# Two preparation steps of the weights, issued on GpSimd or on ScalarE

## The chip, the cores and the metric

One core of a Trainium2 chip runs the whole kernel. Its engines work side by side, each in the order of its own queue: TensorE (PE in the profile, with its weight loads as PEld), VectorE (DVE), ScalarE (ACT), GpSimd (POOL) and SyncE (SP), which issues the DMAs. They wait for each other by semaphores. The metric is the device time of one execution in microseconds (us): the median of the runs shown.

## The reference

Two stages follow each other on `x`, four batches of 12416 rows of 128. The first is attention through 32 inducing points, the second a gated feed-forward layer with 1536 inner columns:

```python
def mab(q, kv):
    s = scale * (q @ kv.transpose(0, 2, 1))
    s = s - s.max(-1, keepdims=True)
    a = np.exp(s)
    a /= a.sum(-1, keepdims=True) + 1e-09
    return a @ kv
h = mab(I, x)                 # the inducing rows look at x
y = mab(x, h)                 # x looks at them
g, val = y @ w_gate, y @ w_val
out = (g * (1.0 / (1.0 + np.exp(-g))) * val) @ w_out
```

All inputs and outputs are float32. Inside the kernel the three weights arrive as pairs of 32-bit words and are made into float32 on the chip.

## The kernel before

Since `y = a @ h`, the kernel multiplies the weights of gate and value by `h` first (32 rows a batch) and then runs them on the attention weights `a`. The output side is a product of a high and a low part, each of the type fp32r: three matmuls in L735 to L737 (`h_hi` with `wo_lo`, `h_hi` with `wo_hi`, `h_lo` with `wo_hi`).

The work after the first 66 us is a loop over slots (25 column groups of 12 tiles for each of the four batches). A slot has two matmuls into `gv` (L696, L697), the silu on ScalarE (L702), the product on VectorE (L710), the cast to `h_hi` (L718), the subtraction for `h_lo` (L720, mostly on GpSimd) and the three output matmuls of an earlier tile. The first column group of batch 0 (`whole`) is done differently: its output matmul is a single one in float32 (L732).

The change lies in what comes before that loop, from about 28 to 66 us, where the weights are made ready. They come in nine pieces of 512 columns: J0 to J5 for gate and value, o0 to o2 for the output. The class `Piece` (from L170) has one method for each step:

- `X` (L186, ScalarE) scales the high words into a work buffer `t`; `sh` (L189, VectorE) shifts and masks `t`; `jn` (L192, VectorE) joins in the sign bit and reads two operands from SBUF.
- `low` (L183) scales the low words by 2^-29, from uint32 to int32, in place with a step of two words.
- `add` (L195, GpSimd) adds `t` and the scaled low words as integers. The result is a piece of `wgv_sb`, or for o0 to o2 the float32 weight that L732 uses.
- For o0 to o2 only, `hi` (L198) casts that weight to `wo_hi` (fp32r), and `lo` (L201, GpSimd) subtracts it to give `wo_lo`.

The order of all this is written out by hand, in the string `SECOND` and the table `FIRST`. Each token is a call, and each engine runs its own instructions in the order of the tokens. The part that the prediction speaks of most:

```python
jn:J3 pa:2 f:2 g:1 add:o0 m:0 pk:2 X:J4 sum:1 f:3 pm:2 add:J3 rec:1 m:1 g:2 X:o1 k:0 pa:3 pc:2 g:3 low:J4 sh:J4 m:2 f:4 f:5 jn:J4 k:1 pk:3 sh:o1 g:4
m:3 no:1:1 pm:3 k:2 at:1 X:J5 sh:J5 pc:3 g:5 low:J5 jn:J5 low:o1 jn:o1 add:J4 pa:4 add:J5 f:6 m:4 pk:4 m:5 g:6 pb:4 k:3 f:7 pa:5 m:6 add:o1 ah:1:1 f:8
al:1:0 g:7 X:o2 pk:5 sh:o2 g:8 low:o2 k:4 pm:5 f:9 jn:o2 pc:5 k:5 f:10 sp:1 m:7 k:6 m:8 f:11 g:9 add:o2 k:7 m:9 g:10 g:11 m:10 m:11 hi:o0 lo:o0 hi:o1
```

The other tokens: `pa:i` is the matmul that projects piece Ji (L403, TensorE), with `pk`, `pb`, `pm` and `pc` (L406 to L417) to split the result; `f`, `g`, `m`, `k` are the matmuls, silu, product and output matmul (L732) of a tile of the first column group; `sum`, `rec`, `no` (L472, on GpSimd), `at`, `ah`, `al`, `sp` normalise the attention weights of the next group, transpose, split and spread them; `z0` to `z8` make the attention weights of the first group (L531 is `z5`, L541 is `z6`). `ld:o1` and `ld:o2` reload buffers that `add:J0` and `add:J1` have read.

Of the kernel before, what the change touches and what calls it, by code (L numbers as in the profile page):

```python
# [11 lines left out]
AF = mybir.ActivationFunctionType  # L12
ALU = mybir.AluOpType
AX = mybir.AxisListType
U32 = mybir.dt.uint32
I32 = mybir.dt.int32
# [94 lines left out]
def induced_set_attention_then_swiglu(ctx: ExitStack, tc: tile.TileContext, xt, xn, ind, wgv, wo, out):  # L111
    nc = tc.nc
# [49 lines left out]
    wo_hi = const.tile([P, DFF], F32R, name="wo_hi")  # L162
# [7 lines left out]
    class Piece:  # L170
# [9 lines left out]
            nc.sync.dma_start(out=raw, in_=(wo if k == "o" else wgv)[:, 2 * WP * i:2 * WP * i + 2 * WP].rearrange("p (n w) -> p n w", w=2))  # L180

        def low(self):
            nc.scalar.activation(out=self.lw.bitcast(I32), in_=self.lw, func=AF.Copy, scale=2.0 ** -29)  # L183

        def X(self):
            nc.scalar.activation(out=self.t.bitcast(F32), in_=self.hw.bitcast(F32), func=AF.Copy, scale=2.0 ** -112)  # L186
# [8 lines left out]
            nc.gpsimd.tensor_add(out=self.w.bitcast(I32), in0=self.t.bitcast(I32), in1=self.lw.bitcast(I32))  # L195

        def hi(self):
            nc.scalar.copy(out=wo_hi[:, self.cs], in_=self.w)  # L198

        def lo(self):  # L200
            nc.gpsimd.tensor_sub(out=wo_lo[:, self.cs], in0=self.w, in1=wo_hi[:, self.cs].bitcast(F32))  # L201
# [14 lines left out]
    def attention(b, one, xn0=None, xt0=None):  # L216
# [19 lines left out]
        def load_xt(q, lo=0, hi=None):  # L236
            if lo == 0:
                if xn0 is not None and q >= NXT and q not in st.xt:
                    st.xt[q] = xt0.tile([P, max(CH), NG, 32], F32, name="xt0")
                else:  # L240
                    st.xt[q] = xtp.tile([P, max(CH), NG, 32], F32, name="xt_sb")
            hi = CH[q] if hi is None else hi
            nc.sync.dma_start(
                out=st.xt[q][:, lo:hi],
                in_=xt[b, :, P * (CH0[q] + lo):P * (CH0[q] + hi)].rearrange("c (i j r) -> c i j r", j=NG, r=32))
# [10 lines left out]
        def load_xn(q, lo=0, hi=None):  # L256
            hi = CH[q] if hi is None else hi
            nc.sync.dma_start(out=rows(q)[:, lo:hi], in_=xn[b, :, CH0[q] + lo:CH0[q] + hi, :])
# [160 lines left out]
        def proj_round(i, ev=nc.vector.tensor_copy):  # L419

            weights()
            ps = ps_gv.tile([P, 512], F32, name="gv")
            for j in range(NG):
                at = PC * (NG * i + j)
                nc.tensor.matmul(out=ps[32 * j:32 * j + 32, :PC], lhsT=st.hT[:, 0:M], rhs=wgv_sb[:, at:at + PC], start=True, stop=True)  # L425
            hi, lo = [eTp.tile([P, W], F32R, name="eT")[:, :PC] for _ in range(2)]
            ev(out=hi, in_=ps[:, :PC])
            nc.vector.tensor_sub(out=lo, in0=ps[:, :PC], in1=hi.bitcast(F32))
            st.pw[i] = hi, lo
# [418 lines left out]
```

## Time and profile before

| what | us |
|---|---|
| median of 3 runs | 1397.06 (1396.88 to 1397.12) |
| the profiled execution | 1398.15 |
| its span in the trace | 1396.4 |
| PE busy | 1381.0 |
| ACT busy | 1254.6 |
| POOL busy | 1193.8 |
| DVE busy | 1184.5 |

The trace holds every instruction of one execution, with start and duration. The span runs from its first to its last instruction; the execution's own time is 1.75 us longer. Rows of groups give the line, engine, operation, output and inputs, shape, count, then the busy time in us and the mean in ns, then the idle time of the engine just before. Rows in order of time give the start and the duration in us. Rows of one line give the duration in ns as minimum, median and maximum. An instruction's start can lie a little before the end of the one before it on its engine, since they overlap.

### The profile page before, as it was taken

What the parts mean: (1) busy time and instruction counts of PE and PEld (TensorE: products, weight loads), DVE (VectorE), ACT (ScalarE), POOL (GpSimd) and SP (SyncE); (2) the same over time, 40 slices, a digit from 0 to 9 for tenths busy, and PEclk for the clock granted to TensorE, in tenths of its full rate; (3) what the DMA queues carried; (4) which work ended last, traced back from release to release, by engine and by line L of the source; (5) the groups of instructions that cost most, each with busy time, mean ns of one, the idle gap of its engine ahead of it and who ended that gap; (6) DMA issues with size and microseconds to landing.
All of it is one profiled execution on the core that took longest, in us unless ns stands there. A gap on an engine that the chain in (4) does not pass through costs nothing.

```text
span 1396.4 us, 24926 instructions
## 1 busy us (share of the span) xinstructions
PE 1381.0 (99%) x7452; PEld 1177.1 (84%) x7452; DVE 1184.5 (85%) x2080; ACT 1254.6 (90%) x2388; POOL 1193.8 (85%) x995
## 2 busy tenths in 40 slices
PE   8999999999999999999999999999999999999998
PEld 6577788889987887799998788789999888889998
DVE  5788878988888888988888878988888888888887
ACT  4888898889998898999999888799999999999997
POOL 1589868989998878899999878889989999999997
PEclk9999999999999999999999999999999999999999
DMA  9224432312133443121124424321111111111110
GB/s 368 86 75 151 161 111 95 112 55 72 39 119 114 143 137 117 51 74 38 41 60 128 145 85 139 110 73 56 41 43 45 33 44 46 34 45 40 43 43 22
DMA packets 50822, 119.80 MB, mean 86 GB/s; under 512 B 11392, under 2 KB 28288, under 8 KB 50688
## 3 DMA queue, kind: packets, MB, share of 16 engines
q1 hardware_dynamic: 50688, 118.22, 25.9%
q8 instruction: 59, 0.97, 0.3%
q14 instruction: 75, 0.61, 0.1%
HBM read 62.87 MB, written 25.43 MB: 63 GB/s over the span
## 4 chain that ended last, share of the span: by engine, by line
PE 92%; ACT 3%; DVE 2%; DMA 1%; issue 1%; POOL 0%; SPq 0%; DVEq 0%; ACTq 0%
PE gv L697 17%; PE o L737 17%; PE o L735 17%; PE gv L696 17%; PE o L736 17%; PE gv L275 2%; ACT h_hi L718 1%; ACT silu L702 1%; DMA xt<-xt 1%; PE o L323 1%; PE o L732 1%; DVE h L710 1%; PE o L275 1%; POOL h_lo L720 0%; PE gv L425 0%
## 5 line engine op out<-in xcount | busy, mean ns | idle before, releaser
L720 POOL TENSOR_TENSOR h_lo<-h,h_hi 128x512 fp32r<-128x512 f32 (+1 forms) x890 | 1098.1, 1258 | 153.8 <-ACT h_hi L718 100.1
L702 ACT ACTIVATE silu<-gv 128x512 f32<-128x512 f32 (+1 forms) x1200 | 705.2, 588 | 63.1 <-PE gv L696 54.5
L710 DVE TENSOR_TENSOR h<-gv,silu 128x512 f32<-128x512 f32 (+1 forms) x891 | 593.9, 668 | 149.6 <-ACT silu L702 86.1
L718 ACT CAST h_hi<-h 128x512 fp32r<-128x512 f32 (+1 forms) x788 | 476.8, 605 | 44.1 <-DVE h L710 34.5
L696 PE MATMUL gv<-stack,tw 128*128 128x512 f32 (+1 forms) x1200 | 453.8, 378 | 2.4 <-DVE stack L548 0.8
L697 PE MATMUL gv<-stack,tw 128*128 128x512 f32 (+1 forms) x1200 | 450.7, 376 | 3.6 <-ACT silu L702 1.8
L737 PE MATMUL o<-h_lo,wo_hi 128*128 128x512 f32 (+1 forms) x1188 | 446.0, 375 | 0.1
L735 PE MATMUL o<-h_hi,wo_lo 128*128 128x512 f32 (+1 forms) x1188 | 445.4, 375 | 0.0
L736 PE MATMUL o<-h_hi,wo_hi 128*128 128x512 f32 (+1 forms) x1188 | 442.8, 373 | 0.0
L697 PEld LDWEIGHTS gv<-stack,tw 128*128 128x128 f32 x1200 | 226.6, 189 | 41.6 <-ACT silu L702 9.6
L696 PEld LDWEIGHTS gv<-stack,tw 128*128 128x128 f32 x1200 | 226.7, 189 | 35.0 <-issue 3.1
L735 PEld LDWEIGHTS o<-h_hi,wo_lo 128*128 128x128 f32 x1188 | 224.5, 189 | 35.1 <-issue 12.1
L737 PEld LDWEIGHTS o<-h_lo,wo_hi 128*128 128x128 f32 x1188 | 224.4, 189 | 33.6 <-POOL h_lo L720 8.8
L736 PEld LDWEIGHTS o<-h_hi,wo_hi 128*128 128x128 f32 x1188 | 224.5, 189 | 23.4
L710 DVE TENSOR_TENSOR gv<-gv,silu 128x512 f32<-128x512 f32 (+1 forms) x297 | 201.3, 678 | 35.4 <-ACT silu L702 33.3
L720 DVE TENSOR_TENSOR h_lo<-gv,h_hi 128x512 fp32r<-128x512 f32 (+1 forms) x297 | 197.4, 665 | 1.0 <-ACT h_hi L718 0.3
L718 ACT CAST h_hi<-gv 128x512 fp32r<-128x512 f32 (+1 forms) x294 | 168.0, 571 | 7.5 <-DVE gv L710 5.0
L744 DVE COPY ob<-o 128x512 f32<-128x512 f32 (+1 forms) x100 | 66.3, 663 | 0.6 <-PE o L737 0.6
L718 DVE CAST h_hi<-h 128x512 fp32r<-128x512 f32 (+1 forms) x103 | 52.6, 511 | 0.0
L488 POOL TENSOR_TENSOR a_lo<-aT,a_hi 128x480 fp32r<-128x480 f32 (+2 forms) x26 | 33.5, 1288 | 0.0
L195 POOL TENSOR_TENSOR wgv_sb<-s_all 128x512 int32<-128x512 int32 x2 | 2.9, 1490 | 29.5 <-ACT s_all L183 29.5
L472 POOL TENSOR_TENSOR s_all<-s_all,sm 128x512 f32<-128x512 f32 (+2 forms) x27 | 25.9, 960 | 0.0
(155 smaller groups left out, 481.7 us busy)
## 6 DMA issues: line engine op xcount, KB each, us to landing
xt_sb<-xt SPq DMA_DIRECT2D x32, 896.0 KB, 5.2
xn_sb<-xn SPq DMA_DIRECT2D x18, 896.0 KB, 5.6
out<-ob SPq DMA_DIRECT2D x52, 256.0 KB, 2.0
out<-ob SPq DMA_DIRECT2D x48, 240.0 KB, 2.0
stack<-a_hi SPq DMA_DIRECT2D x96, 64.0 KB, 2.0
stack<-a_lo SPq DMA_DIRECT2D x96, 64.0 KB, 2.0
stack<-a_hi SPq DMA_DIRECT2D x96, 60.0 KB, 2.0
stack<-a_lo SPq DMA_DIRECT2D x96, 60.0 KB, 2.0
```

The source lines that it names most:

```text
L275: nc.tensor.matmul(out=ps[32 * j:32 * j + 32, 32 * (lo - b0):32 * (hi - b0)], lhsT=lhsT, rhs=st.xt[q][:, lo - CH0[q]:hi - CH0[q], j, :], s ...
L488: eng.tensor_sub(out=st.al[q][:, :n], in0=st.at[q][:, :n], in1=st.ah[q][:, :n].bitcast(F32))
L696: nc.tensor.matmul(out=u.g[:, :n], lhsT=st.w[:, wcol(0, t)], rhs=rhs, start=True, stop=True)
L697: nc.tensor.matmul(out=u.v[:, :n], lhsT=st.w[:, wcol(1, t)], rhs=rhs, start=True, stop=True)
L702: nc.scalar.activation(out=u.s[:, :u.n], in_=u.g[:, :u.n], func=AF.Silu)
L710: nc.vector.tensor_mul(out=u.h[:, :n], in0=u.v[:, :n], in1=u.s[:, :n])
L718: (nc.vector.tensor_copy if u.cast_dve else nc.scalar.copy)(out=u.hi[:, :n], in_=u.h[:, :n])
L720: eng.tensor_sub(out=u.lo[:, :n], in0=u.h[:, :n], in1=u.hi[:, :n].bitcast(F32))
L735: nc.tensor.matmul(out=o[:, :n], lhsT=wo_lo[:, ws], rhs=hi, start=(t == 0), stop=False)
L736: nc.tensor.matmul(out=o[:, :n], lhsT=wo_hi[:, ws], rhs=hi, start=False, stop=False)
L737: nc.tensor.matmul(out=o[:, :n], lhsT=wo_hi[:, ws], rhs=lo, start=False, stop=(t == NT - 1))
L744: nc.vector.tensor_copy(out=ob[:, :n], in_=o[:, :n])
```

## The change

Two methods of `Piece` issue their instruction on GpSimd instead of ScalarE. `low` is called nine times and becomes a `tensor_scalar` with one multiplication; `hi` is called three times and becomes a `tensor_copy`. The order of the tokens stays as it is, so each instruction takes the place in GpSimd's queue that its token has.

```diff
         def low(self):
-            nc.scalar.activation(out=self.lw.bitcast(I32), in_=self.lw, func=AF.Copy, scale=2.0 ** -29)
+            nc.gpsimd.tensor_scalar(out=self.lw.bitcast(I32), in0=self.lw, scalar1=2.0 ** -29, scalar2=None, op0=ALU.mult)
...
         def hi(self):
-            nc.scalar.copy(out=wo_hi[:, self.cs], in_=self.w)
+            nc.gpsimd.tensor_copy(out=wo_hi[:, self.cs], in_=self.w)
```

## The prediction

> **What bounds the kernel now.** I read the page first: the busy times, then the chain of work that ended last.
>
> ```profile
> span 1396.4 us, 24926 instructions
> ...
> PE 1381.0 (99%) x7452; PEld 1177.1 (84%) x7452; DVE 1184.5 (85%) x2080; ACT 1254.6 (90%) x2388; POOL 1193.8 (85%) x995
> ...
> PE 92%; ACT 3%; DVE 2%; DMA 1%; issue 1%; POOL 0%; SPq 0%; DVEq 0%; ACTq 0%
> ```
>
> PE is the bound: 1381.0 of 1396.4 us busy, 92% of the chain. ScalarE (ACT) is 90% busy but holds 3% of the chain, so work taken off ACT pays only where PE waits for ACT. Next I looked where the moved instructions stand, and how busy each engine is there (in the last three rows: the stretch, then PE, PEld, DVE, ACT and POOL busy, the granted clock, DMA).
>
> ```profile
> L183 ACT ACTIVATE s_all<-s_all x4: 669/690/840, 30.7 to 53.4; 128x512 int32<-128x512 uint32 x4
> L183 ACT ACTIVATE xn_sb<-xn_sb x3: 657/832/844, 34.0 to 48.5; 128x512 int32<-128x512 uint32 x3
> L183 ACT ACTIVATE tw<-tw x2: 667/667/667, 32.9 to 33.4; 128x512 int32<-128x512 uint32 x2
> ```
>
> ```profile
> L198 ACT CAST wo_hi<-s_all x2: 621/622/622, 58.1 to 61.1; 128x512 fp32r<-128x512 f32 x2
> ```
>
> ```profile
> 45.07 0.83 ACT L183 ACTIVATE xn_sb<-xn_sb 128x512 int32<-128x512 uint32 x1
> ```
>
> ```profile
> 28.00:36.00 8.00, 6.96 (x60) 4.68 (x56) 7.06 (x20) 6.38 (x12) 2.94 (x2) 0.79 0.93 354
> 36.00:42.00 6.00, 4.85 (x44) 2.71 (x37) 5.16 (x11) 5.45 (x11) 3.01 (x3) 1.00 0.31 104
> 42.00:56.00 14.00, 13.90 (x38) 6.77 (x38) 12.16 (x22) 13.74 (x25) 7.39 (x6) 1.00 0.10 24
> ```
>
> All twelve (nine scalings, three casts) lie between 30.7 and 61.8 us, once per run; the remaining 1335 us of the span hold none. From 42 to 56 us PE is busy 13.90 of 14.00 us although ACT is busy 13.74: ACT is full there, yet PE loses 0.10 us in all. Between 36 and 42 us PE idles 1.15 us, but between the scaling at 34.0 us and the one at 45.07 us ACT runs none, so none of that idling is theirs. The gain to be had is therefore at most the 0.10 us, and I now ask what GpSimd (POOL) pays.
>
> **The change part by part.** Removed from ACT: nine scalings at about 0.69 us and three casts at 0.62 us, some 8 us of an engine that PE does not wait for. Value: 0 to 0.1 us.
>
> Added to POOL: nine tensor_scalar and three copies, 128x512, one input each. The trace has no such form on POOL. The nearest rows:
>
> ```profile
> L195 POOL TENSOR_TENSOR wgv_sb<-tw 128x512 int32<-128x512 int32 x2 | 2.6, 1293 | 1.8 <-ACT tw L186 1.8
> ...
> masks.py:199 POOL TENSOR_SCALAR_AFFINE_SELECT ident<-ident 128x128 f32<-128x128 f32 x1 | 0.3, 292 | 0.1
> masks.py:197 POOL MEMSET ident<- 128x128 f32 x1 | 0.2, 204 | 0.0
> ...
> L141 POOL MEMSET odd<- 128x1 f32 x1 | 0.1, 98 | 0.0
> ```
>
> A fixed part of 98 ns shows at one element. Writing alone grows by (204 - 98)/127 = 0.83 ns an element: 0.52 us at 512, the lower bound. One input with arithmetic grows by (292 - 98)/127 = 1.53 ns: 0.88 us. Two inputs take 1.29 us, the upper bound (a slow conversion of uint32 could go beyond; see the rivals). I take 0.87 us, by the affine select, which also has one input.
>
> The GPSIMD Engine Reference of the Trainium skill (§ 4.1 Engine selection) calls one-input work roughly line-rate on GpSimd, which would be near the lower bound; its § 3.1 gives 769 ns for 512 elements in its best loop. By that figure the sum below would be about 0.3 us smaller. Its advice in § 4.1 to keep elementwise work off GpSimd speaks against the change.
>
> Now POOL's queue where it is tight. In the written order it becomes, after add:J3: low:J4, no:1, low:J5, low:o1, add:J4, add:J5, add:o1, low:o2, add:o2. Ahead of add:J4 there stood only no:1; now three scalings stand there too, and low:o1 serves a piece needed later. PE's matmul on J4 (L403, pa:4) follows add:J4. The rows of before on POOL, PE and DVE:
>
> ```profile
> 40.28 1.52 POOL L195 TENSOR_TENSOR xn_sb<-xn_sb 128x512 int32<-128x512 int32 x1 [2.64 <-ACT sl L552]
> 41.76 1.30 POOL L195 TENSOR_TENSOR wgv_sb<-tw 128x512 int32<-128x512 int32 x1
> 43.02 1.25 POOL L472 TENSOR_TENSOR s_all<-s_all,sm 128x512 f32<-128x512 f32 x1
> 45.98 1.29 POOL L195 TENSOR_TENSOR wgv_sb<-xn_sb 128x512 int32<-128x512 int32 x1 [1.71 <-ACT xn_sb L183]
> 49.47 1.30 POOL L195 TENSOR_TENSOR wgv_sb<-xn_sb 128x512 int32<-128x512 int32 x1 [2.20 <-ACT xn_sb L183]
> ```
>
> ```profile
> 47.96 1.02 PE L403 MATMUL gv<-wgv_sb,hT 128*128 128x512 f32 x2
> ...
> 51.02 0.67 PE L403 MATMUL gv<-wgv_sb,hT 128*128 128x512 f32 x1
> ```
>
> ```profile
> 39.97 0.68 DVE L192 SCALAR_TENSOR_TENSOR tw<-tw 128x512 uint32<-128x512 uint32 x1
> ...
> 42.93 0.43 DVE L189 TENSOR_SCALAR xn_sb<-xn_sb 128x512 uint32<-128x512 uint32 x1
> ...
> 44.03 0.79 DVE L192 SCALAR_TENSOR_TENSOR xn_sb<-xn_sb 128x512 uint32<-128x512 uint32 x1
> ```
>
> The reader is to see three things. First, add:J5 ended at 50.77 and its matmul began at 51.02: 0.25 us from POOL to PE. So pa:4 at 47.96 wants add:J4 done by 47.71; it ended at 47.27, with 0.44 us to spare. Second, add:o0 took 1.52 us while the DVE's join (two inputs from SBUF) ran until 40.65; alone it takes 1.29. POOL and DVE wait for each other on some operations. Third, DVE's shifts (L189, 0.42 us for 512 elements) and joins (L192) fall in the very stretch in which POOL will now run without a pause. What that can do stands later in the trace:
>
> ```profile
> L718 DVE CAST h_hi<-h x103: 398/421/2699, 76.1 to 1390.5; 128x512 fp32r<-128x512 f32 x54, 128x480 fp32r<-128x480 f32 x49
> ```
>
> ```profile
> 571.98 2.70 DVE L718 CAST h_hi<-h 128x512 fp32r<-128x512 f32 x1
> ```
>
> ```profile
> 572.18 1.31 POOL L720 TENSOR_TENSOR h_lo<-h,h_hi 128x512 fp32r<-128x512 f32 x1
> 573.43 0.97 POOL L458 TENSOR_TENSOR s_all<-s_all,mx2b 128x448 f32<-128x448 f32 x1
> ```
>
> A DVE cast with a median of 0.42 us, as fast as the shifts, took 2.70 us and ended 0.28 us after POOL's run of back-to-back instructions (573.43 + 0.97 = 574.40).
>
> The skill's page SBUF — State Buffer (Who interferes with whom) has the rule: DVE's 2-port operations, and those with two SBUF inputs, take a port pair that GpSimd needs, exclusively for a whole instruction. The two rows agree. That rule alone would cost each such shift or join up to one POOL instruction.
>
> The sum, with port turns (whoever holds it finishes, then the other goes). add:J3 ends at 43.05 as before. The shift of J4 keeps its place to 43.36; low:J4 43.36 to 44.23; join J4 waits, 44.23 to 44.85; no:1 (about 1.05 undisturbed: its 1.25 less the 0.2 it waited for the shift) to 45.9; shift o1 to 46.3; low:J5 to 47.17; low:o1 to 48.04; shift J5 waits, to 48.4; add:J4 to 49.7; pa:4 at 49.95. PE is in order and has nothing to put in the gap, so it loses 49.95 - 47.96 = **2.0 us**. The next ones then have room: join J5 to 50.3, join o1 to 50.95, add:J5 to 52.2, pa:5 ready at 52.45 against 51.02 + 2.0 = 53.0.
>
> The casts: add:o2, the row at 54.35 below, would end near 57.6 (54.35 + 1.29 + 2.0); cast and subtraction of o0 take 0.87 + 1.25, so wo_lo is there at 59.7, of o1 at 61.8.
>
> ```profile
> 64.70 0.38 PE L735 MATMUL o<-h_hi,wo_lo 128*128 128x512 f32 x1
> ```
>
> ```profile
> 34.32 0.36 DVE L531 TENSOR_TENSOR z<-z,zs 128x128 f32<-128x128 f32 x1
> ```
>
> ```profile
> 35.76 0.43 PE L541 MATMUL gv<-ident,z 128*32 128x128 f32 x8
> ```
>
> ```profile
> 54.35 1.29 POOL L195 TENSOR_TENSOR s_all<-s_all 128x512 int32<-128x512 int32 x1 [2.34 <-ACT s_all L183]
> ```
>
> PE first uses wo_lo at 64.70 + 2.0, five microseconds later: cost 0; without that cover each would cost its 0.87. The early scalings fill POOL's idle time before 31 us and between 34.5 and 40.3 us; they can delay DVE by one POOL instruction, about 1 us, and z is ready 1.08 us (35.76 - 34.68) before PE takes it: cost 0, up to 1. No DMA is issued by what moves; the reloads behind add:J0 and add:J1 keep their time. After 66 us nothing differs, and PE carries the shift to the end.
>
> The profiled execution took 1398.15 us with a span of 1396.4, and stood 1.09 above the median. So span 1398.4, execution 1400.15, **median 1399.1 us**.
>
> **Rivals.**
>
> B, nothing worth telling is lost: POOL is late by itself only. Without any waiting on DVE, add:J4 would end at 43.05 + 3 x 0.87 + 1.05 + 1.29 = 48.0, pa:4 at 48.25: +0.3, 1397.4 us. For it speaks that the shift at 42.93 got in between two POOL instructions at once; against it the 2.70 us cast.
>
> C, clearly slower: GpSimd's scaling costs more than two inputs do, or DVE is shut out for a whole run of POOL. Each 0.1 us of price adds 0.3 through the three scalings ahead of add:J4; it passes 0.2% at about 1.15 us a scaling. At 1.7 us it is 2.0 + 3 x 0.83 = +4.5, 1401.6 us; at 2.3 us +6.3, 1403.4. A DVE shut out from 43.05 until low:o1 ends at 46.7 adds 0.4 to the sum, as does a late z up to 1. For it: integers in and out on POOL are unmeasured here. A PE stall could also bring the clock down: it was granted 0.79 over 28 to 36 us, after 1.04 us of idling, which is 8 x 0.21 = 1.7 us more; against that, 1.15 us of idling from 36 to 42 was followed by 1.00.
>
> D, the other side, a small gain: at the lower price of 0.52 us and with DVE winning the port, add:J4 ends at 43.05 + 1.56 + 1.05 + 1.29 = 46.95, earlier than before, and pa:5 no longer waits for low:J5 on ACT. PE gets its 0.10 us back and at best 0.3 more between 40 and 42: 1396.7 to 1397.0 us. It decides from a price below 0.77 (47.71 = 45.39 + 3 x 0.77). A gain over 0.2% needs 2.8 us, more than PE idles in the whole stretch after 36 us (1.15 + 0.10).
>
> **How the numbers follow.** Forecast 45%, B 17%, C 33%, D 5%. I call 0.2% (2.8 us) what a measurement can tell. B and D lie within it; of the forecast's own spread (+1 to +3.3 by prices of 0.6 to 1.29) a fifth lies beyond. So slower 0.33 + 0.08 = 0.41, faster 0.03 (taken from D for what I have not seen), same 0.56. The range takes D's better end and C up to a scaling of 2.3 us: 1396.8 to 1403.5 us; the forecast's own is 1398.1 to 1400.4.
>
> **What would show it.** A POOL row for L183 gives the price: 0.87 expected, 0.52 to 1.29 allowed. PE's L403 for J4 should begin near 50 us with POOL L195 as its releaser, DVE's L189 and L192 rows between 43 and 50 us should stretch beyond 0.43 and 0.79 us, and ACT should show idle time there. First L735 near 66.7 us. If L735 comes at 64.7 the loss was absorbed (B or D); if it comes after 68, the price or the lock was worse (C). If it comes at 66.7 and the span has still grown otherwise, something in the steady loop moved, which I hold to be excluded.

## The result, and the profile after

The changed kernel takes 1404.13 us (median of 4 runs, 1402.64 to 1406.76), the kernel before 1396.97 us in the runs beside it: a ratio of 1.0052, 95% interval 1.004 to 1.0064. It is 7.2 us slower. That lies outside the stated range, which ended at 1403.5, and on the side of rival C.

The page of the changed kernel, the three lines that answer to those of before:

```profile
span 1401.7 us, 24929 instructions
...
PE 1382.7 (99%) x7452; PEld 1177.9 (84%) x7452; DVE 1188.3 (85%) x2080; ACT 1249.5 (89%) x2376; POOL 1209.8 (86%) x1007
...
PE 90%; ACT 3%; DMA 2%; DVE 2%; issue 1%; POOL 1%; SPq 0%; DVEq 0%; ACTq 0%
```

ACT's busy time fell by 5.1 us (1254.6 to 1249.5), POOL's rose by 16.0 (1193.8 to 1209.8). By their own rows the twelve instructions took 8.4 us on ACT and take 16.8 on POOL, twice as much.

The moved instructions, now on POOL, and the stretches again (stretch, then PE, PEld, DVE, ACT, POOL busy, granted clock, DMA):

```profile
L183 POOL TENSOR_SCALAR s_all<-s_all x4: 1559/1596/1838, 29.0 to 55.9; 128x512 int32<-128x512 uint32 x4
L183 POOL TENSOR_SCALAR xn_sb<-xn_sb x3: 1634/1640/1641, 38.8 to 48.7; 128x512 int32<-128x512 uint32 x3
L183 POOL TENSOR_SCALAR tw<-tw x2: 1586/1738/1890, 33.7 to 36.8; 128x512 int32<-128x512 uint32 x2
```

```profile
L198 POOL CAST wo_hi<-s_all x2: 609/616/623, 62.1 to 67.8; 128x512 fp32r<-128x512 f32 x2
```

```profile
28.00:36.00 8.00, 6.25 (x78) 3.86 (x70) 6.88 (x17) 4.23 (x9) 6.68 (x5) 1.00 0.91 347
36.00:42.00 6.00, 2.62 (x8) 1.29 (x8) 5.94 (x7) 4.80 (x9) 5.58 (x4) 0.99 0.38 122
42.00:56.00 14.00, 11.54 (x27) 5.85 (x28) 11.11 (x21) 8.00 (x15) 12.66 (x10) 0.88 0.00 1
```

A scaling takes 1.6 us, the cast 0.62. From 42 to 56 us ACT falls from 13.74 to 8.00 us busy and POOL rises from 7.39 to 12.66; PE, which lost 0.10 us there before, now loses 2.46, and its clock is 0.88 where it was 1.00.

Where PE waits, in order of time:

```profile
33.68 1.13 PE L403 MATMUL gv<-wgv_sb,hT 128*128 128x512 f32 x2 [0.86 <-POOL wgv_sb L195]
...
36.77 1.13 PE L403 MATMUL gv<-wgv_sb,hT 128*128 128x512 f32 x2 [0.81 <-POOL wgv_sb L195]
40.00 0.48 PE L696 MATMUL gv<-stack,tw 128*128 128x512 f32 x1 [2.11 <-DVE stack L548]
...
41.87 2.07 PE L403 MATMUL gv<-wgv_sb,hT 128*128 128x512 f32 x2 [0.51 <-POOL wgv_sb L195]
...
53.41 1.12 PE L403 MATMUL gv<-wgv_sb,hT 128*128 128x512 f32 x2 [2.46 <-POOL wgv_sb L195]
...
69.93 0.38 PE L735 MATMUL o<-h_hi,wo_lo 128*128 128x512 f32 x1
```

The last row is the start of the steady loop: 69.93 instead of 64.70, 5.23 us later. From there to the end of the span it is 1331.8 us (1401.7 - 69.93) against 1331.7 before. The whole difference of the two traces lies ahead of it, in two places: the waits up to 42 us, and the wait of 2.46 us for the sum of J4. PE takes J2 1.94 us later than before (41.87 against 39.93), J3 2.88 (46.66 against 43.78) and J4 5.45 (53.41 against 47.96). (The span of this one execution grew by 5.3 us and the median by 7.2: the profiled execution before stood 1.2 us above the median of these runs, this one 0.6 below its own.)

Two rows of the kernel before, for J2 and J3:

```profile
39.93 1.02 PE L403 MATMUL gv<-wgv_sb,hT 128*128 128x512 f32 x2
...
43.78 1.02 PE L403 MATMUL gv<-wgv_sb,hT 128*128 128x512 f32 x2
```

In the changed kernel TensorE ran at half its clock between J2 and J3, which is why the matmuls of J2 took 2.07 us instead of 1.02:

```profile
41.83:45.24 3.41, 3.37 (x6) 2.06 (x7) 3.34 (x8) 1.77 (x4) 2.39 (x2) 0.50 0.00 0
```

POOL's queue and DVE at the first of these places:

```profile
29.00 3.27 POOL L183 TENSOR_SCALAR s_all<-s_all 128x512 int32<-128x512 uint32 x2 [26.97 <-DMA s_all<-wgv]
32.35 1.28 POOL L195 TENSOR_TENSOR wgv_sb<-s_all 128x512 int32<-128x512 int32 x1
33.71 1.59 POOL L183 TENSOR_SCALAR tw<-tw 128x512 int32<-128x512 uint32 x1
35.38 1.34 POOL L195 TENSOR_TENSOR wgv_sb<-s_all 128x512 int32<-128x512 int32 x1
36.80 1.89 POOL L183 TENSOR_SCALAR tw<-tw 128x512 int32<-128x512 uint32 x1
38.77 1.63 POOL L183 TENSOR_SCALAR xn_sb<-xn_sb 128x512 int32<-128x512 uint32 x1
40.48 1.34 POOL L195 TENSOR_TENSOR wgv_sb<-tw 128x512 int32<-128x512 int32 x1
```

```profile
34.74 0.83 DVE L189 TENSOR_SCALAR tw<-tw 128x512 uint32<-128x512 uint32 x1
35.50 1.77 DVE L458 TENSOR_TENSOR s_all<-s_all,mx2a 128x512 f32<-128x512 f32 x1
37.19 1.12 DVE L192 SCALAR_TENSOR_TENSOR tw<-tw 128x512 uint32<-128x512 uint32 x1
...
40.60 1.50 DVE L189 TENSOR_SCALAR tw<-tw 128x512 uint32<-128x512 uint32 x1
```

The shift at 34.74 ends at 35.57, 0.27 us after the scaling beside it (33.71 + 1.59 = 35.30); the one at 40.60 ends at 42.10, 0.28 us after the sum (41.82). Both take 0.42 us undisturbed. L458 took 0.68 us before and takes 1.77:

```profile
34.93 0.68 DVE L458 TENSOR_TENSOR s_all<-s_all,mx2a 128x512 f32<-128x512 f32 x1
```

The first shift, L458 and the join at 37.19 stand in DVE's queue ahead of the operations that make the stack (L548, the attention weights that L696 reads); the shift at 40.60 stands ahead of the next two joins.

POOL, however, has no gap from 29.00 us to the end of the sum of J2 at 41.82, and PE takes J2 at 41.87. Of the waits up to 42 us the one for the stack is the longest (2.11 us), but the one for this sum ends last: with an earlier stack PE would have waited longer for the sum. What DVE's delays do cost POOL is its one gap ahead of the sum of J4, 1.03 us from 41.82 to 42.85, in which it waits for a join behind the shift of 40.60.

And at the second place, POOL between the sums of J3 (44.42) and J4 (52.07):

```profile
44.42 1.30 POOL L195 TENSOR_TENSOR wgv_sb<-tw 128x512 int32<-128x512 int32 x1
45.80 1.64 POOL L183 TENSOR_SCALAR xn_sb<-xn_sb 128x512 int32<-128x512 uint32 x1
47.52 1.10 POOL L472 TENSOR_TENSOR s_all<-s_all,sm 128x512 f32<-128x512 f32 x1
48.71 1.64 POOL L183 TENSOR_SCALAR xn_sb<-xn_sb 128x512 int32<-128x512 uint32 x1
50.43 1.56 POOL L183 TENSOR_SCALAR s_all<-s_all 128x512 int32<-128x512 uint32 x1
52.07 2.53 POOL L195 TENSOR_TENSOR wgv_sb<-xn_sb 128x512 int32<-128x512 int32 x2
```

That is the queue of the prediction, low:J4, no:1, low:J5, low:o1, add:J4, without a pause. Only its scalings are almost twice as long. And DVE's joins get in beside them; this one runs within the scaling of 45.80 in its undisturbed time:

```profile
46.52 0.67 DVE L192 SCALAR_TENSOR_TENSOR xn_sb<-xn_sb 128x512 uint32<-128x512 uint32 x1
```

### The profile page after: what moved, and what is told of

The parts are those of the page before. It is cut to its first block, busy times and chain, and to the rows that moved or that the text cites. A ratio compares the mean times of both kernels' runs of the same rounds, so it can differ in the third digit from the quotient of the medians.

```text
span 1401.7 us, 24929 instructions
## 1 busy us (share of the span) xinstructions
PE 1382.7 (99%) x7452; PEld 1177.9 (84%) x7452; DVE 1188.3 (85%) x2080; ACT 1249.5 (89%) x2376; POOL 1209.8 (86%) x1007
## 4 chain that ended last, share of the span: by engine, by line
PE 90%; ACT 3%; DMA 2%; DVE 2%; issue 1%; POOL 1%; SPq 0%; DVEq 0%; ACTq 0%
PE o L737 17%; PE gv L697 17%; PE o L735 17%; PE gv L696 17%; PE o L736 17%; PE gv L275 2%; ACT silu L702 1%; ACT h_hi L718 1%; PE o L323 1%; DMA s_all<-wgv 1%; DMA xt<-xt 1%; DVE h L710 1%; PE o L275 1%; PE o L732 1%; POOL h_lo L720 0%
## 5 line engine op out<-in xcount | busy, mean ns | idle before, releaser
L718 ACT CAST h_hi<-h 128x512 fp32r<-128x512 f32 (+1 forms) x788 | 476.7, 605 | 44.0 <-DVE h L710 34.5
L696 PE MATMUL gv<-stack,tw 128*128 128x512 f32 (+1 forms) x1200 | 455.5, 380 | 3.3 <-DVE stack L548 2.1
L735 PE MATMUL o<-h_hi,wo_lo 128*128 128x512 f32 (+1 forms) x1188 | 445.4, 375 | 0.0
L696 PEld LDWEIGHTS gv<-stack,tw 128*128 128x128 f32 x1200 | 227.1, 189 | 35.2 <-DVE stack L548 2.9
L735 PEld LDWEIGHTS o<-h_hi,wo_lo 128*128 128x128 f32 x1188 | 224.5, 189 | 35.1 <-issue 12.1
L710 DVE TENSOR_TENSOR gv<-gv,silu 128x512 f32<-128x512 f32 (+1 forms) x297 | 201.2, 677 | 35.9 <-ACT silu L702 34.1
L183 POOL TENSOR_SCALAR s_all<-s_all 128x512 int32<-128x512 uint32 x4 | 6.6, 1648 | 27.2 <-DMA s_all<-wgv 27.0
```

Of the source, the lines that this page charges most:

```text
L696: nc.tensor.matmul(out=u.g[:, :n], lhsT=st.w[:, wcol(0, t)], rhs=rhs, start=True, stop=True)
L710: nc.vector.tensor_mul(out=u.h[:, :n], in0=u.v[:, :n], in1=u.s[:, :n])
L718: (nc.vector.tensor_copy if u.cast_dve else nc.scalar.copy)(out=u.hi[:, :n], in_=u.h[:, :n])
L735: nc.tensor.matmul(out=o[:, :n], lhsT=wo_lo[:, ws], rhs=hi, start=(t == 0), stop=False)
```

## The experiments

My theory after the result: the scaling's price on GpSimd was sized wrong, and it acts in two ways, by making the sums late in POOL's queue and by keeping DVE from the port. Rivals: the casts; POOL's lateness alone; the written order; half-clock stretches of TensorE.

**Scalings only, and casts only.** One half of the change each.

```diff
 # e1_scale_only: hi as before
+            nc.gpsimd.tensor_scalar(out=self.lw.bitcast(I32), in0=self.lw, scalar1=2.0 ** -29, scalar2=None, op0=ALU.mult)
             nc.scalar.copy(out=wo_hi[:, self.cs], in_=self.w)
 # e2_cast_only: low as before
             nc.scalar.activation(out=self.lw.bitcast(I32), in_=self.lw, func=AF.Copy, scale=2.0 ** -29)
+            nc.gpsimd.tensor_copy(out=wo_hi[:, self.cs], in_=self.w)
```

> Only the nine scalings are on GpSimd; the three casts stay on ScalarE. Theory (the scaling's price of 1.6 us on GpSimd makes the loss, in front of the matmuls of the pieces and through VectorE's waits): the same loss as the whole change, +5 to +9 us in the median, with TensorE waiting about 2.5 us for the sum of J4 and about 2 us for VectorE's stack. Rival (the casts crowd GpSimd's queue as well): at most +4 us.

> Only the three casts are on GpSimd; the nine scalings stay on ScalarE. Theory: the casts cost 0.62 us each on GpSimd at a place where the low part of the output weights has some 5 us in hand, so the time stays within 0.5 us of the kernel before. Rival (casts crowd the queue): +1 us or more.

Scalings only: 1405.29 us against 1397.07, ratio 1.0058 (1.0043 to 1.0073). Casts only: 1397.67, ratio 1.0002 (0.9992 to 1.0012), no difference that can be told (0.6 us in the medians, just past the 0.5 of the theory). The scalings make the loss.

**What the scaling's price is made of.** Extra instructions on GpSimd at the start of the kernel before.

```diff
+    for _ in range(3):
+        nc.gpsimd.tensor_scalar(out=b2, in0=a, scalar1=0.5, scalar2=None, op0=ALU.mult)
+        nc.gpsimd.tensor_scalar(out=b2.bitcast(I32), in0=a.bitcast(U32), scalar1=0.5, scalar2=None, op0=ALU.mult)
+        nc.gpsimd.tensor_scalar(out=st2, in0=st2, scalar1=0.5, scalar2=None, op0=ALU.mult)
+        nc.gpsimd.tensor_scalar(out=st2.bitcast(I32), in0=st2.bitcast(U32), scalar1=0.5, scalar2=None, op0=ALU.mult)
+        nc.gpsimd.tensor_scalar(out=half2.bitcast(I32), in0=half2.bitcast(U32), scalar1=0.5, scalar2=None, op0=ALU.mult)
+        nc.gpsimd.tensor_copy(out=wo_hi[:, 0:512], in_=a)
+        nc.gpsimd.tensor_copy(out=b2.bitcast(I32), in_=a.bitcast(U32))
...
```

> The kernel before with extra instructions on GpSimd at its start, on tiles not yet in use, three of each: a multiplication by a scalar, 128x512, (a) float32 to float32, (b) uint32 to int32, both contiguous, (c) float32 and (d) uint32 to int32 with a step of two words in place, (e) as (d) with 256 elements; (f) a copy from float32 to fp32r, (g) a copy from uint32 to int32, (h) a multiplication float32 to int32, (i) uint32 to float32. Its time says nothing. If the integer types make the price: (b) and (d) 1.6 us, (a) and (c) 0.5 to 0.9 us. If the step of two words makes it: (c) and (d) 1.6 us, (a) and (b) 0.5 to 0.9. If the multiplication by a scalar is itself slow: all of (a) to (d) about 1.6 us, while the copies (f) and (g) stay near 0.62.

Its rows by line, in the order of the diff without the third and the last, which agree with their neighbours (duration in ns as minimum, median, maximum):

```profile
L170 POOL TENSOR_SCALAR wgv_sb<-wgv_sb x3: 1492/1497/1514, 3.8 to 29.9; 128x512 f32<-128x512 f32 x3
```

```profile
L171 POOL TENSOR_SCALAR wgv_sb<-wgv_sb x3: 1488/1492/1740, 6.7 to 31.5; 128x512 int32<-128x512 uint32 x3
```

```profile
L173 POOL TENSOR_SCALAR wgv_sb<-wgv_sb x3: 1564/1572/1573, 8.2 to 24.1; 128x512 int32<-128x512 uint32 x3
```

```profile
L174 POOL TENSOR_SCALAR wgv_sb<-wgv_sb x3: 899/910/922, 10.3 to 27.1; 128x256 int32<-128x256 uint32 x3
```

```profile
L175 POOL CAST wo_hi<-wgv_sb x3: 617/617/636, 9.7 to 29.4; 128x512 fp32r<-128x512 f32 x3
```

The multiplication by a scalar is itself slow: 1.49 us with every pair of types (the two mixed pairs, not shown, took 1.495 and 1.494), more than the 1.29 us of a sum of two tensors. The step of two words adds 0.08 us and the integer types nothing. The copy takes 0.62 us. From 256 to 512 elements the scaling grows by (1572 - 910)/256 = 2.6 ns an element.

**The three scalings ahead of the sum of J4, and the five before them.** Only some pieces are scaled on GpSimd; the casts stay on ScalarE.

```diff
         def low(self):
+            if self.k + str(self.i) in ('J4', 'J5', 'o1'):       # e4: ('J0', 'J1', 'J2', 'J3', 'o0')
+                nc.gpsimd.tensor_scalar(out=self.lw.bitcast(I32), in0=self.lw, scalar1=2.0 ** -29, scalar2=None, op0=ALU.mult)
+            else:
+                nc.scalar.activation(out=self.lw.bitcast(I32), in_=self.lw, func=AF.Copy, scale=2.0 ** -29)
```

> Only the scalings of J4, J5 and o1 are on GpSimd, the three that stand ahead of the sum of J4; the others and the casts stay on ScalarE. By the price measured (1.6 us) and turns at the port my sum gives 2.0 + 3 x 0.73 = +4.2 us, by GpSimd's queue alone 43.05 + 3 x 1.6 + 1.05 + 1.29 + 0.25 - 47.96 = +2.5 us. Theory: +2.5 to +4.2 us, TensorE's whole wait at the matmul of J4. Rival (most of the loss comes earlier, from VectorE held up at 35 to 42 us): under +1.5 us.

> Only the scalings of J0, J1, J2, J3 and o0 are on GpSimd; J4, J5, o1, o2 and the casts stay on ScalarE. The trace of the changed kernel shows TensorE waiting 2.11 us for VectorE's stack, where the kernel before waited 0.82, and 0.5 to 0.9 us for each of the sums of J0, J1 and J2. Theory (VectorE's subtraction took 1.77 instead of 0.68 us and the shifts up to 1.50 instead of 0.42 because GpSimd holds the port): +1 to +2.5 us. Rival (these waits are filled by idle time that was there before): within 0.5 us.

The last three: 1401.24 us, +4.2 (1.0031, 1.0019 to 1.0043), at the upper end of the theory. The first five: 1400.54, +3.5 (1.0026, 1.0016 to 1.0036), more than the theory gave. Together 7.6 us, where all scalings cost 8.2 in the same runs: the two places add up. PE with the last three (lines are shifted by 3 in these two kernels), the stretch behind its wait, then PE's waits with the first five:

```profile
49.30 2.07 PE L406 MATMUL gv<-wgv_sb,hT 128*128 128x512 f32 x2 [2.60 <-POOL wgv_sb L198]
```

```profile
49.30:52.70 3.40, 3.40 (x7) 1.83 (x7) 0.68 (x1) 1.29 (x3) 2.42 (x2) 0.59 0.00 0
```

```profile
PE gv L406 <- POOL wgv_sb L198: 2.2, 3, 0.8
PE gv L699 <- DVE stack L551: 2.1, 1, 2.1
```

With the last three, PE's wait is 2.60 us, which is the sum by POOL's queue alone (2.5). The matmuls of J4 then take 2.07 us instead of 1.02, at a clock of 0.59 over the 3.4 us behind the wait, and J5 follows J4 by 4.27 us (53.57 - 49.30) instead of 3.06 (51.02 - 47.96). With the first five the waits are those of the changed kernel up to 42 us, the stack's 2.1 us among them. Here too POOL has no gap, from 28.27 us to the end of the sum of J2 at 41.13, PE takes J2 at 41.18, and its matmuls run at half clock (2.08 us). So the trace puts this loss on POOL's queue, where the theory for this run had put it on the port.

**Queue or port.** GpSimd is held up at the places of the scalings by fills of a tile not yet in use; the scalings are on ScalarE, as before. Once with two long fills at each place, once with 20 fills of one element, once with 10, once with 10 at the first five places alone.

```diff
         def low(self):
             nc.scalar.activation(out=self.lw.bitcast(I32), in_=self.lw, func=AF.Copy, scale=2.0 ** -29)
+            nc.gpsimd.memset(wo_lo.bitcast(F32), 0.0)            # e7: two long fills
+            nc.gpsimd.memset(wo_lo[:, 0:128].bitcast(F32), 0.0)
...
+            for _ in range(20):                                  # e8; 10 in e11, and in e12 for J0 to J3 and o0
+                nc.gpsimd.memset(wo_lo[:, 0:1].bitcast(F32), 0.0)
```

> The kernel before (scalings and casts on ScalarE), with two fills of a tile not yet in use on GpSimd at each place where the changed kernel has a scaling: 1536 and 128 elements, together about 1.6 us by the fills in the trace (204 ns for 128, 98 for 1). GpSimd's queue is as late as in the changed kernel, but these instructions read nothing. Theory (port): VectorE's joins and its subtraction keep their 0.7 us and the loss is smaller than the changed kernel's, +2 to +4.8 us. Rival (the lateness of GpSimd's queue alone makes the whole loss): +5 to +7 us, as in the changed kernel.

> The kernel before with 20 fills of one element (about 0.1 us each in the trace, 1.5 to 2 us together) on GpSimd at each place where the changed kernel has a scaling. GpSimd's queue is as late as in the changed kernel, but between two short fills VectorE can take the port. Theory (two causes, queue and port): VectorE's shifts stay near 0.42 us and at most 0.7, TensorE's wait for the stack falls back to about 0.8 us, the wait for the sum of J4 stays near 2.5 us: +2 to +4.5 us, as with the last three scalings alone. Rival (GpSimd's lateness is the whole loss): +5 to +7 us, and the stack is late as in the changed kernel. Second rival (the shifts are shut out by any unbroken run on GpSimd, however short its pieces): shifts up to 2 us and +5 to +7 us.

> The kernel before with 10 fills of one element at each place of a scaling: 20 of them took 3.33 us, so 10 make 1.67 us, the price of the scaling, while VectorE's shifts and joins kept their 0.42 and 0.69 us among them. GpSimd's queue is as late as in the changed kernel, the port is free. Theory (queue and port both): what is left is the queue's part, 43.05 + 3 x 1.67 + 1.05 + 1.29 + 0.25 - 47.96 = +2.7 us for the sum of J4, and no wait above 0.9 us for the stack: +2.2 to +4 us, against the changed kernel's +7. Rival (the queue alone): +6 us or more.

> The same 10 fills, but only at the places of J0, J1, J2, J3 and o0, whose real scalings on GpSimd cost +3.5 us. Theory (the early loss is VectorE shut out from the port): within +0.7 us of the kernel before. Rival (the early loss is GpSimd's lateness for the sums of J0 to J2): +2.5 us or more.

GpSimd is not as late in these runs as was meant. The fills of J0 and J1 wait for nothing and ran before 9 us, in its idle time, while the real scalings of J0 and J1 began at 29.00 us with their data. Only the later places are held up.

Two long fills: 1402.77 us, +5.8 (1.0048, 1.0031 to 1.0065), in the rival's range. But this run doesn't tell the two apart, because fills that read nothing shut DVE out all the same, as its rows show (DVE, then POOL):

```profile
34.55 2.83 DVE L191 TENSOR_SCALAR tw<-tw 128x512 uint32<-128x512 uint32 x1
```

```profile
34.50 1.29 POOL L197 TENSOR_TENSOR wgv_sb<-s_all 128x512 int32<-128x512 int32 x1
35.73 1.38 POOL L184 MEMSET wo_lo<- 128x1536 f32 x1
```

The shift waited through the sum and through the fill, and ended at 37.38, 0.27 us after it. My theory had taken writes to be harmless.

Twenty fills: 1412.0 us, +14.9 (1.0108, 1.0093 to 1.0123), outside every range given, since they made POOL late by 3.3 us a place and not 1.6. It still settles one point. Through all of it DVE's shifts kept their duration:

```profile
L191 DVE TENSOR_SCALAR s_all<-s_all x4: 415/420/426, 29.7 to 66.4; 128x512 uint32<-128x512 uint32 x4
L191 DVE TENSOR_SCALAR xn_sb<-xn_sb x3: 419/427/439, 37.6 to 53.3; 128x512 uint32<-128x512 uint32 x3
L191 DVE TENSOR_SCALAR tw<-tw x2: 418/419/420, 34.3 to 37.9; 128x512 uint32<-128x512 uint32 x2
```

A run of fills on POOL does not shut DVE out if its pieces are short; long instructions can.

Ten fills, the scaling's price: 1402.45 us, +5.5 (1.004, 1.0025 to 1.0055), above the theory's +2.2 to +4 and under the rival's +6. Ten fills at the first five places: 1398.03, +1.0 (1.0009, 0.9999 to 1.0018), just past the theory's 0.7. PE at the sum of J4 with ten fills everywhere, then with ten at the first five places L458 (here L461):

```profile
50.81 1.88 PE L405 MATMUL gv<-wgv_sb,hT 128*128 128x512 f32 x2 [3.04 <-POOL wgv_sb L197]
```

```profile
L461 DVE TENSOR_TENSOR s_all<-s_all,mx2a x1: 1794/1794/1794, 34.1 to 34.1; 128x512 f32<-128x512 f32 x1
```

So at the first five places the real scalings cost 3.5 us and the short fills 1.0. That does not show that the other 2.5 us come from the port, because POOL was not equally late: counted from TensorE's matmuls on `hn` (L389 in the kernel before), the sum of J2 began 7.1 us later in the kernel before, 9.9 with ten fills at the first five places, and 11.7 with the real scalings there. No run here separates the two at this place; the trace of the first five puts POOL's queue last. Even the 1.0 is not free of the port: the subtraction stretched to 1.79 us again, now against the sum of J1, which the fills had pushed beside it. At the sum of J4 the lateness alone is enough: PE waits 3.04 us and then runs its matmuls at a reduced clock (1.88 instead of 1.02).

**The price in place.** The changed kernel with a copy of zeros in place of each scaling; the low three bits of the weights are left out.

```diff
         def low(self):
-            nc.gpsimd.tensor_scalar(out=self.lw.bitcast(I32), in0=self.lw, scalar1=2.0 ** -29, scalar2=None, op0=ALU.mult)
+            nc.gpsimd.tensor_copy(out=self.lw.bitcast(I32), in_=wo_lo[:, :WP].bitcast(I32))
```

> The changed kernel with each scaling replaced by a copy on GpSimd, 0.62 us instead of 1.6, into the same words. It leaves the scaling of the low words out (zeros are copied in, so the weights lose their lowest three bits). Theory (the price is what my sum had wrong; the sum itself holds): by that sum 2.0 - 3 x 0.25 = +1.25 us, so +0.5 to +2 us, no wait of more than 1.5 us for the sum of J4. Rival (any reading instruction in these places shuts VectorE out, whatever it costs): +3 us or more.

1398.91 us against 1397.15: +1.8 (1.0012, 1.0003 to 1.0022), in the theory's range. PE waits 0.15 us for the sum of J4, so what is left is lost elsewhere; PE waits 0.63 us for z, where it did not before, behind a join of DVE that took 1.66 us beside the sum of J0:

```profile
48.70 1.13 PE L404 MATMUL gv<-wgv_sb,hT 128*128 128x512 f32 x2 [0.15 <-POOL wgv_sb L196]
```

Same queue, same order, a shorter instruction in each place, and three quarters of the loss are gone.

**The order.** In the changed kernel each scaling is moved in the written order to just ahead of its own sum.

```diff
-jn:J3 pa:2 f:2 g:1 add:o0 m:0 pk:2 X:J4 sum:1 f:3 pm:2 add:J3 rec:1 m:1 g:2 X:o1 k:0 pa:3 pc:2 g:3 low:J4 sh:J4 m:2 f:4 f:5 jn:J4 k:1 pk:3 sh:o1 g:4
-m:3 no:1:1 pm:3 k:2 at:1 X:J5 sh:J5 pc:3 g:5 low:J5 jn:J5 low:o1 jn:o1 add:J4 pa:4 add:J5 f:6
+jn:J3 pa:2 f:2 g:1 low:o0 add:o0 m:0 pk:2 X:J4 sum:1 f:3 pm:2 low:J3 add:J3 rec:1 m:1 g:2 X:o1 k:0 pa:3 pc:2 g:3 sh:J4 m:2 f:4 f:5 jn:J4 k:1 pk:3 sh:o1 g:4
+m:3 no:1:1 pm:3 k:2 at:1 X:J5 sh:J5 pc:3 g:5 jn:J5 jn:o1 low:J4 add:J4 pa:4 low:J5 add:J5 f:6
...
```

> The changed kernel, with each scaling moved in the written order to just ahead of its own sum, so that no scaling of a later piece stands ahead of the sum that TensorE needs next. Theory (queue order): the wait of 2.46 us for the sum of J4 falls below 1 us, and the loss falls from +5 to +7 us to +1 to +3.5 us. Rival (the price and the port decide, whatever the order): the loss stays above +4.5 us.

1403.81 us, +6.9 (1.0049, 1.0034 to 1.0064): the rival. PE's waits from 28 to 75 us:

```profile
PE gv L403 <- POOL wgv_sb L195: 2.6, 2, 2.3
PE gv L541 <- DVE z L531: 2.4, 1, 2.4
PE o L732 <- POOL s_all L195: 1.6, 1, 1.6
PE gv L696 <- DVE stack L548: 1.0, 1, 1.0
```

The waits moved (z is now late, and the sums of J3 and o1) and did not shrink. This order doesn't mend it: from 28.4 to 60.5 us POOL's gaps of more than 0.1 us come to 1.3 us, so it lacks the time.

**The changed kernel again.**

> The changed kernel again, unaltered, beside the two others on one chip: for a second profile and a second set of times. If half-clock stretches of TensorE in the gaps make the spread of 4 us between its runs, the clock and the time of the runs go together, 1.7 us for each stretch of 3.4 us at half clock. If the turns at the port make it, the time varies at one clock.

1405.04 us, ratio 1.0056 (1.0041 to 1.0071). Its four runs with their mean granted clock: 1403.21 (0.997), 1404.98 (0.997), 1405.1 (0.998), 1406.16 (0.997). Two runs at 0.997 lie 2.95 us apart, where a step of 0.001 in the mean clock is 1.4 us of the span; the profiled one of the four had a half-clock stretch twice as long as the first profile's (0.50 from 38.63 to 45.45 us) and was the fastest; and the reordered kernel varied from 1402.87 to 1404.71 at a clock of 0.999 to 1.0. Half-clock stretches are therefore not the whole of what spreads the runs. They may be part of it: over both sets of the changed kernel the runs at 0.998 took 1402.64 to 1405.1 us, those at 0.996 and 0.997 1403.21 to 1406.76. That the turns at the port make the rest fits, but no run shows it.

## Why the prediction was wrong

- **What bounds the kernel: right.** PE carried every microsecond lost to the end (5.23 at the first L735, 5.3 in the span), and 5.1 us off ACT bought nothing.
- **The price of a scaling: the step that failed.** The prediction took "0.87 us, by the affine select, which also has one input", with 1.29 us, two inputs, as upper bound. It is 1.6 us, above that bound; the row nearest in form was the wrong guide, and an operation with one input cost more than one with two. The copy, priced by the same row, is 0.62 us, near the lower bound. One price for both kinds hid that they differ by a factor of 2.5. How much of the 7.2 us the port adds to POOL's lateness stays open; the trace shows it at one point of POOL's queue, the gap of 1.03 us. The line-rate rule of the Trainium skill's GPSIMD Engine Reference (§ 4.1) fits the copy (0.62 us) and not the scaling (1.6 us). The 769 ns that the same page of the Trainium skill gives (§ 3.1) is half of what was measured for the scaling.
- **The sum for J4: the queue was right, the turns at the port were not.** POOL's instructions stood in the trace in the order given. But the sum also has 1.69 us in which POOL waits for DVE (0.31 + 0.62 + 0.40 + 0.36), and in the trace POOL paused for less than 0.1 us at a time. That the wait came out near the forecast (2.46 against 2.0) is luck: a price too low by 0.73 us three times over stood against turns that did not come. By the measured price the sum gives 2.0 + 3 x 0.73 = 4.2 us, and the last three scalings alone cost +4.2; that agreement is luck as well, since what was measured is a wait of 2.60 us, the queue alone, and matmuls at half clock behind it. With the copy's price the sum gives 1.25, measured +1.8, but PE lost only 0.15 of it at J4.
- **The early scalings: wrong, for the price again.** They were to "fill POOL's idle time before 31 us and between 34.5 and 40.3 us", cost 0, up to 1. They cost +3.5. From POOL's first start at 29.00 us, five scalings and two sums would let the sum of J2 begin at 35.9 at the earliest with 0.87 us, ahead of the 36.35 before, but at 39.6 with 1.6 us; it began at 40.48. So the idle time was full, and PE waited for POOL. The prediction raised the price in rival C, but replayed only the J4 queue with it. It also had the port in the 2.70 us cast and applied it only at J4: it checked z (which was in time) and neither the stack nor the join for which POOL then waited 1.03 us.
- **The casts: right**, nothing.
- **The rivals.** C happened, for its first reason and near a price that it names ("at 1.7 us" 1401.6). Its sign, a first L735 after 68 us, came (69.93). Its clock stall, weighed as an extra, came too, behind the waits up to 42 us and not at J4, and the early loss was missing from it. D needed a price below 0.77. The advice of the Trainium skill's GPSIMD Engine Reference (§ 4.1) against elementwise work on GpSimd held.
- **The range** ended at 2.3 us a scaling through the J4 queue alone. It was short by the early place, not by the price.

## What to carry to other kernels

Price an instruction on another engine by its own operation, and where no row has it keep both ends far apart: on GpSimd a copy and a scalar multiplication of the same tile were 0.62 and 1.5 us. When work moves to an engine that looks half idle, replay the whole stretch at the upper price, and ask for every neighbour that shares a port with it, not only at the tightest queue. An engine's full busy share (13.74 of 14 us on ACT) says nothing of what relieving it is worth as long as another engine sets the end.

## What the hardware showed that I had not expected

- GpSimd's multiplication by a scalar takes 1.49 us for 512 elements whatever the types, more than its sum of two tensors (1.29 us); with a step of two words it grows by 2.6 ns an element.
- A long fill on GpSimd, which reads nothing, shut a VectorE shift out for its whole length, as did the sum before it (2.83 instead of 0.42 us together), while a run of one-element fills did not (0.42). The page SBUF — State Buffer (Who interferes with whom) of the Trainium skill says that 2-port operations contend with GpSimd; the trace agrees.
- By the same section of the Trainium skill an operation with two SBUF inputs contends with a reading GpSimd instruction, under an exclusive lock. Beside the scalings the trace does not agree: the join at 46.52 ran within one in its undisturbed time (0.67), and the join at 37.19 began while the scaling of 36.80 to 38.69 ran, and ended at 38.31, before it: it was slowed (1.12 instead of 0.69), not shut out. Beside a sum of two tensors L458 did wait: it ended at 37.27, 0.55 us after the sum (36.72).
- The stretch of some 3.4 us at about half clock is there before and after. Before, it fell between 28 and 36 us, where TensorE runs its warm-up transposes; in the changed kernel it fell behind the waits up to 42 us (0.50 from 41.83), and with the last three scalings moved on the matmuls behind the wait for J4 (0.59 from 49.30 us). The reordered kernel waited 2.4 and 2.3 us and had no such stretch (1.00 from 25 to 75 us). A wait can cost more than its length.
